# Channel attention with an ELU feed-forward network: thirteen row buffers for batch 0, three early groups of batch 1, and key-query matmuls placed between others

## The chip, the core and the metric

The kernel runs on one core of one Trainium2 chip. The time is device microseconds of one execution; before the change it is 2296.42 us, the median of three runs (2296.3 to 2297.59). The profile is one more execution on the chip, with every instruction's start and end. Engines in it: PE is TensorE's matmul, PEld its weight load, DVE is VectorE, ACT ScalarE, POOL GpSimd, SP SyncE, which issues the DMAs. L12 is line 12 of the kernel.

## The reference

Four batches (B = 4) of N = 6080 rows with C = 256 channels. Attention is over channels: the key-query product is 256 x 256 for a batch and sums over all rows, so nothing of a batch's softmax can start before its last row is there. An ELU network of width 2048 follows.

```python
def _attn_ref(q, k, v, tau) -> np.ndarray:
    qn = q / (np.linalg.norm(q, axis=1, keepdims=True) + 1e-06)
    kn = k / (np.linalg.norm(k, axis=1, keepdims=True) + 1e-06)
    s = kn.transpose(0, 2, 1) @ qn / tau
    s = s - s.max(-1, keepdims=True)
    a = np.exp(s)
    a /= a.sum(-1, keepdims=True) + 1e-09
    return (v @ a).astype(np.float32)

def _moe_ref(x, w_in, w_out) -> np.ndarray:
    h = x @ w_in
    alpha = 1.0
    g = np.where(h > 0.0, h, alpha * (np.exp(np.minimum(h, 0.0)) - 1.0))
    return (g @ w_out).astype(np.float32)
```

Inputs are fp32, the two weight matrices arrive as 64-bit floats.

## The kernel before, in words

The order of the products is changed: for each batch `W' = a @ w_in` (256 x 2048) is made once, and then `h = v @ W'`, the ELU and `g @ w_out` run over the batch's tokens. Most products are split: each fp32 operand becomes a high part and a rest (`split`, a cast on ACT and a subtraction on DVE, L80), and three fast matmuls (high x high, high x rest, rest x high) stand for one. In the head the products are plain fp32 instead; there each matmul shows as two instructions.

**Head (L436 to L502, in an order written out by hand for TensorE and SP).** Rows of q and k come in groups: one group is two rows of every partition, 256 KB of q and 256 KB of k. 6080 rows are 47 a partition and 64 left over; so there are 24 groups, the last of which, `ragged`, has one full row and the 64 left over. `fill_rows` (L116) issues a group's two DMAs from SP; a group of batch 0 is a tile of tag `raw`, of which there are five buffers, so a load waits until the group five before it has been used. For each group TensorE does `multiply` (L432; four fp32 matmuls, eight instructions, 128x256 each), and `square_rows` adds up squares (ACT squares, L143; DVE adds, L144). Products stand `BEHIND` = 2 groups behind the squares in the order. Among the loads are one piece of `w_in` (1 MB) and the first chunk of v (512 KB). After the last square `norms` (L178 to L207) folds the sums, sums them over the partitions by eight small matmuls (L181), takes the root on ACT and makes a scaled identity `dg`; `spread` (L211) multiplies it out; `softmax` and `transpose_a` (L244, copies to `aT` on ACT, L248) follow; `wp_item` (L277) makes the first quarter of W'. The last two groups' products of batch 0 stand behind the norms' matmuls. As a filler, `EARLY` = 2 groups of batch 1 are loaded into a scratch buffer `scr` and multiplied in plain fp32 into a PSUM tile `pe`, partly behind the spread and partly behind the transposes.

The pool tag `wp` has four buffers of 16 KB a partition. Two hold the W' of one batch (`new_wp`), two (`scr`, `scr_r`) serve as scratch in the head and as the next batch's W' later. W' of batch 0 is written at the end of the head and not earlier.

**Main loop (L613 on).** Its steps are pairs (chunk c of 512 or 496 tokens, slice f of 128 of the 2048 hidden channels). A batch has 12 chunks (eight of 512 tokens, then four of 496) of 16 slices. A step is `h_item` (six matmuls, L319 to L321), the ELU on ACT and DVE (`elu`), a split of its result g (L81, L82) and, three steps later (`LAG`), `out_item` (six matmuls, L356 to L358). The first M = 4 chunks go in pieces of slices, because the rest of W' is still being made. Other work is hung on steps: `at(step, fn)` puts it behind the step's own work, `free` ones (the conversions of the weights from 64 bits, `to_f32`) only behind the first softmax (`issue_after(attended)`). For the next batch's attention each group is loaded, squared and split at a step x + 2, and its key-query matmuls (`gram_item`, L157; two 512-wide and two 256-wide for each half of the channels) stand as one run behind the steps x + 4 and x + 5. Outside the head the order on each engine is the scheduler's, from a model of its own and the order of the program as priority.

Of the kernel before, what the change touches and what calls it, by code (L numbers as in the profile page):

```python
# [7 lines left out]
F32 = mybir.dt.float32  # L8
# [20 lines left out]
def channel_attention_then_elu_ffn(ctx: ExitStack, tc, q, k, vT, tau, w_in, w_out, outT):  # L29
# [127 lines left out]
    def gram_item(hl, gram, ct, first, last):  # L157

        pg = gram[ct]
        cs = slice(ct * P, ct * P + P)  # L160
        for r in range(2):
            nc.tensor.matmul(  # L162
                pg, hl[:, 0, 1, r, cs], hl[:, :, 0, r, :], start=(first and r == 0), stop=False
            )
            nc.tensor.matmul(  # L165
# [74 lines left out]
    def transpose_a(b, a):  # L240
# [4 lines left out]
        if b == 0:  # L245
            aT = work.tile([P, KT, C], F32, tag="aT", bufs=1, name=f"aT_{b}")
            for jt in range(KT):
                nc.scalar.copy(aT[:, jt], pt[:, jt])  # L248
        else:
            aT = work.tile([P, 2, KT, C], F32R, tag="aT", bufs=1, name=f"aT_{b}")  # L250
            split(aT[:, 0], aT[:, 1], pt)
# [99 lines left out]
    def out_item(c, f, g, po):  # L351
        n = span(c)[2]
        hi, lo = (g[:, x, 0:n] for x in range(2))
        for dt in range(DT):
            o, ds = po[dt][:, 0:n], slice(dt * P, dt * P + P)
            nc.tensor.matmul(o, wo[:, f, 0, ds], hi, start=first(c, f), stop=False)  # L356
# [55 lines left out]

    scr = work.tile([P, 2 * F], F32, tag="wp", bufs=2 * KT, name="scr")
# [10 lines left out]
    wps[0] = new_wp(0)  # L424
# [11 lines left out]
    with tc.manual_schedule(engines={nc.tensor.engine, nc.sync.engine}):  # L436
        keep_warm(4)

        warm = tiny.tile([P, 1], F32, name="warm")
        nc.scalar.activation(warm, ones[:, 0:1], AF.Square)  # L440
        ragged = work.tile([P, 2, 2, C], F32, tag="g", bufs=4, name="ragged")
        nc.gpsimd.memset(ragged[:, :, 1, :], 0.0)
        fill_rows(ragged, 0, NG - 1)
        gram0 = [pg0[ct][:, 0, :] for ct in range(KT)]
        none = [False] * KT
        multiply(ragged, 0, gram0, [True] * KT, none)
        raws = {x: load_rows(0, x) for x in range(3)}
# [4 lines left out]
        BEHIND = 2  # L452
        FULL = NG - 1
        raw1 = [scratch(x, k=2 * 2).rearrange("p (t r) c -> p t r c", t=2) for x in range(EARLY)]
        for x in range(FULL):
            if x >= BEHIND:
                raw = raws.pop(x - BEHIND)
                for r in range(2):
                    multiply(raw, r, gram0, none, none)
            if x + 3 < FULL:  # L460
                raws[x + 3] = load_rows(0, x + 3)
            if x == 4:
                fill_left(ragged, 0)
            if x == 6:
                wi64[0] = load_w_in(0)
            if x == 14:
                vraw[0] = load_v(0)
# [4 lines left out]
            if x in (11, 14):  # L472
                convert_w_in(0, wi64[0], [(x - 11) // 3])
        for x in range(EARLY):
            fill_rows(raw1[x], 1, x)
        wo64[0] = load_w_out(0)
        pn, dg, rk, nm, ready = norms(0, acc)
        for x in range(FULL - BEHIND, FULL):
            raw = raws.pop(x)
            for r in range(2):  # L480
                multiply(raw, r, gram0, none, [x == FULL - 1 and r == 1] * KT)
# [9 lines left out]

        pe = ps.tile([P, KT, C], F32, tag="o", bufs=8 - KT - WB, name="pe")
        gram1 = [pe[:, ct, :] for ct in range(KT)]
        parts = [(x, r) for x in range(EARLY) for r in range(2)]
        for x, r in parts[:-1]:
            multiply(raw1[x], r, gram1, [x == 0 and r == 0, False], none)
        aT0 = transpose_a(0, a0)
        x, r = parts[-1]
        multiply(raw1[x], r, gram1, none, [False, True])
# [170 lines left out]
```

## Time and profile before

| | us |
|---|---|
| median of three runs | 2296.42 (2296.3 to 2297.59) |
| the profiled execution, own time | 2297.65 |
| its span, first to last instruction | 2295.9 |
| PE busy | 2284.7 |
| DVE busy | 1532.9 |
| ACT busy | 1484.0 |
| DMA | 118.15 MB, mean 51 GB/s |

A busy PE is not PE at its best: matmuls are pipelined, so a matmul's own duration in the profile (0.39 us for a 512-wide one) is longer than its distance to the next start (0.23 us). Where pace matters, read the starts. Rows of the order of time are: start, duration, engine, line, operation, tile written <- tiles read, shape, count of merged instructions, and in brackets the idle time before them and what ended it.

### The profile page before, as it was taken

What the parts mean: (1) busy time and instruction counts of PE and PEld (TensorE: products, weight loads), DVE (VectorE), ACT (ScalarE), POOL (GpSimd) and SP (SyncE); (2) the same over time, 40 slices, a digit from 0 to 9 for tenths busy, and PEclk for the clock granted to TensorE, in tenths of its full rate; (3) what the DMA queues carried; (4) which work ended last, traced back from release to release, by engine and by line L of the source; (5) the groups of instructions that cost most, each with busy time, mean ns of one, the idle gap of its engine ahead of it and who ended that gap; (6) DMA issues with size and microseconds to landing.
All of it is one profiled execution on the core that took longest, in us unless ns stands there. A gap on an engine that the chain in (4) does not pass through costs nothing.

```text
span 2295.9 us, 27137 instructions
## 1 busy us (share of the span) xinstructions
PE 2284.7 (100%) x10232; PEld 1901.1 (83%) x10232; DVE 1532.9 (67%) x2396; ACT 1484.0 (65%) x2425; POOL 3.4 (0%) x11
## 2 busy tenths in 40 slices
PE   8999999999999999999999999999999999999999
PEld 7878888888888888888888888888888888888887
DVE  6995766676766666666666666666666666666665
ACT  6776666666666666666666666666666666666665
POOL 0000000000000000000000000000000000000000
PEclk9999999999999999999999999999999999999999
DMA  9320111110201111111011111121111000000000
GB/s 320 109 74 19 56 65 55 65 62 37 64 19 56 55 46 56 54 48 52 32 60 37 46 47 56 46 64 46 44 37 55 28 19 28 28 19 10 19 9 19
DMA packets 60948, 118.15 MB, mean 51 GB/s; under 512 B 6032, under 2 KB 15760, under 8 KB 60816
## 3 DMA queue, kind: packets, MB, share of 16 engines
q1 hardware_dynamic: 60816, 116.42, 15.0%
q8 instruction: 80, 1.31, 0.2%
q14 instruction: 52, 0.43, 0.1%
HBM read 89.39 MB, written 27.00 MB: 51 GB/s over the span
## 4 chain that ended last, share of the span: by engine, by line
PE 98%; DMA 1%; DVE 0%; SPq 0%; ACT 0%; issue 0%; ACTq 0%
PE ph L319 15%; PE ph L321 15%; PE po L356 15%; PE po L357 15%; PE po L358 15%; PE ph L320 15%; PE gram L162 3%; PE gram L165 1%; DMA raw<-in_k_dram 1%; PE gram L432 1%; PE pw L277 1%; PE pw L281 0%; PE pw L279 0%; PE pw L280 0%; PE pn L181 0%; DMA raw<-in_q_dram 0%
## 5 line engine op out<-in xcount | busy, mean ns | idle before, releaser
L81 ACT CAST g<-e 128x512 fp32r<-128x512 f32 (+1 forms) x768 | 472.2, 615 | 498.1 <-DVE e L336 270.4
L82 DVE TENSOR_TENSOR g<-e,g 128x512 fp32r<-128x512 f32 (+1 forms) x768 | 525.9, 685 | 342.7 <-ACT g L81 296.4
L356 PE MATMUL po<-g,wo 128*128 128x512 f32 (+1 forms) x1536 | 597.2, 389 | 0.0
L357 PE MATMUL po<-g,wo 128*128 128x512 f32 (+1 forms) x1536 | 595.4, 388 | 0.0
L358 PE MATMUL po<-g,wo 128*128 128x512 f32 (+1 forms) x1536 | 594.9, 388 | 0.0
L319 PE MATMUL ph<-vt,wp 128*128 128x512 f32 (+1 forms) x1472 | 574.3, 390 | 0.0
L321 PE MATMUL ph<-vt,wp 128*128 128x512 f32 (+1 forms) x1472 | 571.7, 388 | 0.0
L320 PE MATMUL ph<-vt,wp 128*128 128x512 f32 (+1 forms) x1472 | 570.2, 387 | 0.0
L332 DVE SCALAR_TENSOR_TENSOR e<-e,ph 128x512 f32<-128x512 f32 (+1 forms) x416 | 283.3, 681 | 304.4 <-ACT e L331 303.7
L330 ACT ACTIVATE e<-ph 128x512 f32<-128x512 f32 (+1 forms) x416 | 247.0, 594 | 167.8 <-PE ph L321 165.1
L358 PEld LDWEIGHTS po<-g,wo 128*128 128x128 f32 x1536 | 288.4, 188 | 59.2
L357 PEld LDWEIGHTS po<-g,wo 128*128 128x128 f32 x1536 | 288.4, 188 | 57.9
L356 PEld LDWEIGHTS po<-g,wo 128*128 128x128 f32 x1536 | 288.3, 188 | 56.8
L319 PEld LDWEIGHTS ph<-vt,wp 128*128 128x128 f32 x1472 | 276.4, 188 | 58.1 <-issue 0.7
L321 PEld LDWEIGHTS ph<-vt,wp 128*128 128x128 f32 x1472 | 276.3, 188 | 56.7
L320 PEld LDWEIGHTS ph<-vt,wp 128*128 128x128 f32 x1472 | 276.7, 188 | 50.9 <-issue 0.7
L331 ACT ACTIVATE e<-e 128x512 f32<-128x512 f32 (+1 forms) x416 | 261.3, 628 | 12.2
L334 ACT ACTIVATE e<-ph 128x512 f32<-128x512 f32 (+1 forms) x352 | 208.5, 592 | 83.4 <-PE ph L321 70.0
L336 DVE TENSOR_TENSOR e<-ph,e 128x512 f32<-128x512 f32 (+1 forms) x352 | 241.0, 685 | 10.5
L335 DVE TENSOR_SCALAR e<-e 128x512 f32<-128x512 f32 (+1 forms) x352 | 148.7, 423 | 53.4 <-ACT e L334 53.1
L144 DVE TENSOR_TENSOR acc<-acc,sq 128x1024 f32<-128x1024 f32 x81 | 98.9, 1221 | 13.7 <-ACT sq L143 13.4
L162 PE MATMUL gram<-qk 128*128 128x512 f32 x280 | 103.1, 392 | 0.0
(106 smaller groups left out, 1176.1 us busy)
## 6 DMA issues: line engine op xcount, KB each, us to landing
raw<-in_q_dram SPq DMA_DIRECT2D x90, 256.0 KB, 2.7
raw<-in_k_dram SPq DMA_DIRECT2D x90, 256.0 KB, 2.9
v<-in_v_dram SPq DMA_DIRECT2D x32, 512.0 KB, 3.4
out_dram<-o SPq DMA_DIRECT2D x56, 256.0 KB, 2.0
v<-in_v_dram SPq DMA_DIRECT2D x16, 496.0 KB, 3.4
out_dram<-o SPq DMA_DIRECT2D x32, 248.0 KB, 2.1
wraw<-w_scr SPq DMA_DIRECT2D x12, 512.0 KB, 3.1
wi<-in_moe_w_in_dram SPq DMA_DIRECT2D x4, 1024.0 KB, 6.7
```

The costliest lines, as they stand in the source:

```text
L81: nc.scalar.copy(hi, src)
L82: nc.vector.tensor_sub(lo, src, hi.bitcast(F32))
L319: nc.tensor.matmul(ph[:, 0:n], wp[kt][:, 0, fs], hi, start=(kt == 0), stop=False)
L320: nc.tensor.matmul(ph[:, 0:n], wp[kt][:, 0, fs], lo, start=False, stop=False)
L321: nc.tensor.matmul(ph[:, 0:n], wp[kt][:, 1, fs], hi, start=False, stop=(kt == KT - 1))
L330: nc.scalar.activation(ev, pv, AF.Relu, scale=-1.0)
L331: x = nc.scalar.activation(ev, ev, AF.Exp, scale=-1.0)
L332: y = nc.vector.scalar_tensor_tensor(ev, ev, -1.0, pv, op0=ALU.add, op1=ALU.max)
L336: y = nc.vector.tensor_tensor(ev, pv, ev, op=ALU.max)
L356: nc.tensor.matmul(o, wo[:, f, 0, ds], hi, start=first(c, f), stop=False)
L357: nc.tensor.matmul(o, wo[:, f, 1, ds], hi, start=False, stop=False)
L358: nc.tensor.matmul(o, wo[:, f, 0, ds], lo, start=False, stop=last(c, f))
```

## The change

- Batch 0's groups get thirteen buffers: eight in the two `wp` buffers that W' of batch 0 takes later (`room`; four groups in each), five of tag `raw`. A load of group x + 13 is issued behind the product of group x. `wps[0]` is made only behind the early items.
- The first loads: k of `ragged` and of groups 0 and 1 is issued by ACT, the rest by SP. Order on SP: ragged, groups 0 to 8, the 64 left-over rows, tau, the piece of w_in, groups 9 to 12, then 13 to 22 as buffers come free, then the first chunk of v (before: behind group 17), the early groups, w_out.
- `BEHIND` = 5; the norms' matmuls now stand ahead of the last group's product only. The second product of `ragged` stands where it did, at x = 9, which is now behind group 4's product instead of group 7's.
- `EARLY` = 3 groups of batch 1; their six parts (one row of a group each) go one ahead of the spread, three behind it, two behind the transposes.
- The squares of the early groups move from behind the softmax to the main loop's steps 1, 2 and 3; what waited for the softmax's last DVE instruction now waits, on ACT, for the last copy to `aT` too.
- `gram_item` becomes a generator; `out_item` issues one of its four matmuls behind each of its own first four. The two halves stand at steps x + 5 and x + 6 instead of behind x + 4 and x + 5.

```diff
-    EARLY = 2
-
-    def fill_rows(raw, b, g):
+    EARLY = 3
+
+    def fill_rows(raw, b, g, queues=(nc.sync, nc.sync)):
...
-            nc.sync.dma_start(
+            queues[t].dma_start(
...
     def gram_item(hl, gram, ct, first, last):
...
-            nc.tensor.matmul(
+            yield nc.tensor.matmul(
                 pg, hl[:, 0, 1, r, cs], hl[:, :, 0, r, :], start=(first and r == 0), stop=False
             )
-            nc.tensor.matmul(
+            yield nc.tensor.matmul(
                 pg[:, 0, :], hl[:, 1, 1, r, cs], hl[:, 0, 0, r, :], start=False, stop=(last and r == 1)
             )
...
-    def out_item(c, f, g, po):
+    def out_item(c, f, g, po, between):
...
             nc.tensor.matmul(o, wo[:, f, 0, ds], hi, start=first(c, f), stop=False)
+            next(between, None)
             nc.tensor.matmul(o, wo[:, f, 1, ds], hi, start=False, stop=False)
+            next(between, None)
             nc.tensor.matmul(o, wo[:, f, 0, ds], lo, start=False, stop=last(c, f))
+            next(between, None)
...
+    room = [work.tile([P, 2 * F], F32, tag="wp", bufs=2 * KT, name=f"room_{x}") for x in range(KT)]
...
+        BEHIND = 5
+        FULL = NG - 1
+        EACH = 2 * F // (2 * KT * C)
+        DEEP = KT * EACH + 5
...
+        def load0(x):
+
+            y = x % DEEP
+            if y < KT * EACH:
+                n = 2 * KT * C
+                raws[x] = room[y // EACH][:, y % EACH * n : (y % EACH + 1) * n].rearrange(
+                    "p (t r c) -> p t r c", t=2, r=2
+                )
+            else:
+                raws[x] = work.tile([P, 2, 2, C], F32, tag="raw", bufs=5, name=f"raw_0_{x}")
+            fill_rows(raws[x], 0, x, (nc.sync, nc.scalar if x < 2 else nc.sync))
+
+        fill_rows(ragged, 0, NG - 1, (nc.sync, nc.scalar))
+        multiply(ragged, 0, gram0, [True] * KT, none)
+        for x in range(3):
+            load0(x)
...
+        for x in range(3, 9):
+            load0(x)
+        fill_left(ragged, 0)
...
+        wi64[0] = load_w_in(0)
+        for x in range(9, DEEP):
+            load0(x)
...
+        def gram0_item(x):
+            raw = raws.pop(x)
+            for r in range(2):
+                multiply(raw, r, gram0, none, [x == FULL - 1 and r == 1] * KT)
+            if x + DEEP < FULL:
+                load0(x + DEEP)
+
         for x in range(FULL):
             if x >= BEHIND:
-                raw = raws.pop(x - BEHIND)
-                for r in range(2):
-                    multiply(raw, r, gram0, none, none)
-            if x + 3 < FULL:
-                raws[x + 3] = load_rows(0, x + 3)
...
+                gram0_item(x - BEHIND)
             square_rows(raws[x], acc, x == 0, sq1 if x % 2 else None)
             if x == 9:
                 square_rows(ragged, acc, False)
                 multiply(ragged, 1, gram0, none, none)
-            if x in (11, 14):
-                convert_w_in(0, wi64[0], [(x - 11) // 3])
+            if x in (12, 15):
+                convert_w_in(0, wi64[0], [(x - 12) // 3])
+        vraw[0] = load_v(0)
         for x in range(EARLY):
             fill_rows(raw1[x], 1, x)
         wo64[0] = load_w_out(0)
+        for x in range(FULL - BEHIND, FULL - 1):
+            gram0_item(x)
         pn, dg, rk, nm, ready = norms(0, acc)
-        for x in range(FULL - BEHIND, FULL):
...
+        gram0_item(FULL - 1)
...
+        early_items(1)
         spread(pn, dg)
...
+        early_items(3)
+        wps[0] = new_wp(0)
+        aT0, copied = transpose_a(0, a0)
+        attended = (attended, copied)
+        early_items(2 * EARLY - 4)
...
-    with tc.issue_after(attended):
+    with tc.issue_after(attended[0]), tc.issue_after(attended[1]):
         convert_w_out(0, wo64[0])
         nc.scalar.copy(early, pe)
-        for x in range(EARLY):
-            square_rows(raw1[x], acc1, x == 0)
...
+    for x in range(EARLY):
+        at(1 + x, lambda x=x: square_rows(raw1[x], acc1, x == 0))
...
-            at(x + 4, lambda b=b, g=g: gram(b, g, 0))
-            at(x + 5, lambda b=b, g=g: gram(b, g, 1))
+            for ct in range(KT):
+                fine[x + 5 + ct] = gram(b, g, ct)
...
-            out_item(c, f, gs.pop(j), pos[c])
+            out_item(c, f, gs.pop(j), pos[c], fine.pop(i, iter(())))
```

`early_items(n)` issues the next n parts of the early groups; a part is the product of one row of a group, two fp32 matmuls.

More of the change, by code (lines that the diff above doesn't have):

```diff
@@ L584, in gram @@
             g0 = first_group(b)
-            gram_item(state[b, "hl", g], state[b, "gram"], ct, g == g0, g == NG - 1)
+            yield from gram_item(state[b, "hl", g], state[b, "gram"], ct, g == g0, g == NG - 1)
         def soft(b):
@@ L629, in channel_attention_then_elu_ffn @@
                 ]
-            out_item(c, f, gs.pop(j), pos[c])
+            out_item(c, f, gs.pop(j), pos[c], fine.pop(i, iter(())))
             if last(c, f):
                 store(c, f, pos.pop(c))
-        with tc.issue_after(attended):
+        with tc.issue_after(attended[0]), tc.issue_after(attended[1]):
             for fn in loose.get(i, ()):
```

48 lines of the change are left out of this document (17 added, 31 removed).

## The prediction

> **What bounds the kernel now.** I read the page's totals first, then the span cut into windows, then TensorE's instructions in order of time.
>
> ```profile
> span 2295.9 us, 27137 instructions
> PE 2284.7 (100%) x10232; PEld 1901.1 (83%) x10232; DVE 1532.9 (67%) x2396; ACT 1484.0 (65%) x2425; POOL 3.4 (0%) x11
> ```
>
> TensorE is the whole path: 11 us of the span are without a matmul. An edit can pay only where TensorE idles, where its clock is down, or where its matmuls follow each other more slowly than their width asks for. The first two lie in the head:
>
> ```profile
> 27.00:45.60 18.60, 18.60 (x87) 16.15 (x85) 17.47 (x21) 13.60 (x15) 0.00 (x0) 1.00 0.93 321
> 45.60:50.70 5.10, 0.14 (x1) 0.00 (x0) 3.33 (x4) 2.58 (x3) 0.00 (x0) 0.95 0.97 320
> 50.70:57.00 6.30, 6.22 (x19) 5.33 (x20) 2.85 (x12) 4.11 (x6) 0.00 (x0) 0.50 1.04 409
> ```
>
> Columns: the window, its length, busy time of PE, weight loads, DVE, ACT, POOL, then granted clock, DMA share, GB/s. TensorE is packed until 45.6, idles 5 us, and then runs 6.3 us at half clock. What it does and waits for, in order of time:
>
> ```profile
> 50.77 1.86 PE L181 MATMUL pn<-ones,acc 128*128 128x1 f32 x8 [5.04 <-DVE acc L178]
> 52.50 5.90 PE L432 MATMUL gram<-raw 128*128 128x256 f32 x16
> 58.24 0.59 PE L211 MATMUL pn<-dg,ones 128*128 128x256 f32 x2
> 58.67 2.75 PE L432 MATMUL pe<-scr 128*128 128x256 f32 x12
> 61.26 0.60 PE L244 MATMUL pt<-ident,a 128*128 128x128 f32 x4
> 62.56 0.81 PE L277 MATMUL pw<-wf,aT 128*128 128x256 f32 x3
> ```
>
> ```profile
> 42.74 4.83 DMA raw<-in_k_dram
> 47.68 1.06 ACT sq L143
> 48.77 1.24 DVE acc L144
> 50.03 0.70 DVE acc L178
> ```
>
> The second fence is the chain of waits. The last k rows land at 47.57; square, addition and fold take 3 us more, and the norm matmuls stand in TensorE's queue ahead of the last two groups' products. So the load bounds the head's end. The product is nearly as long: the twelve instructions from 58.67 to 61.26 are 0.216 us apart, a group of two rows is eight of them (an fp32 matmul is two), 1.73 us. What idling costs beside the wait: the sixteen at 52.50 take until 58.24, 5.74 us, where 16 x 0.216 is 3.46.
>
> The third place is the main loop. In these rows the first column is the start:
>
> ```profile
> 708.93 0.39 PE L319 MATMUL ph<-vt,wp 128*128 128x512 f32 x1
> ...
> 711.65 0.39 PE L162 MATMUL gram<-qk 128*128 128x512 f32 x1
> 711.88 0.28 PE L165 MATMUL gram<-qk 128*128 128x256 f32 x1
> 712.00 0.40 PE L162 MATMUL gram<-qk 128*128 128x512 f32 x1
> 712.23 0.28 PE L165 MATMUL gram<-qk 128*128 128x256 f32 x1
> 712.35 0.40 PE L319 MATMUL ph<-vt,wp 128*128 128x512 f32 x1
> 712.59 0.40 PE L320 MATMUL ph<-vt,wp 128*128 128x512 f32 x1
> ...
> 715.13 0.39 PE L162 MATMUL gram<-qk 128*128 128x512 f32 x1
> ```
>
> A step's twelve 512-wide matmuls take 2.72 us (708.93 to 711.65), 0.227 each; a 256-wide one takes 0.12. After a run of four key-query matmuls the next twelve take 2.78 (712.35 to 715.13), the first of them 0.24, and the run itself 0.70 where 2 x 0.227 + 2 x 0.1135 is 0.68. One run costs about 0.08 us beyond its width. In the 496-wide chunks the slow pace does not end; a step inside the key-query stage takes 2.68 us, one after it 2.64:
>
> ```profile
> 520.04 0.39 PE L319 MATMUL ph<-vt,wp 128*128 128x496 f32 x1
> ...
> 522.72 0.38 PE L319 MATMUL ph<-vt,wp 128*128 128x496 f32 x1
> ```
>
> ```profile
> 612.91 0.38 PE L319 MATMUL ph<-vt,wp 128*128 128x496 f32 x1
> ...
> 615.55 0.38 PE L319 MATMUL ph<-vt,wp 128*128 128x496 f32 x1
> ```
>
> ```profile
> L162 PE MATMUL gram<-qk 128*128 128x512 f32 x280 | 103.1, 392 | 0.0
> ```
>
> 280 records, two to a run, are 140 runs. Some two thirds fall among 512-wide chunks (eight of a batch's twelve), 93 x 0.08 = 7 us; the others leave about 48 steps of each of three batches slow, 144 x 0.04 = 6 us. So about 13 us of the span hang on how these matmuls stand among the others.
>
> **The change, part by part.** *Thirteen buffers.* The loads no longer wait for a buffer, and the first v chunk goes behind all of batch 0's rows. How the rate goes with the queue:
>
> ```profile
> 2.00:9.00 7.00, 6.19 (x17) 4.52 (x16) 0.22 (x1) 2.33 (x4) 0.00 (x0) 1.00 0.90 274
> 30.00:48.00 18.00, 15.74 (x73) 13.50 (x72) 15.98 (x18) 12.32 (x14) 0.00 (x0) 1.00 0.92 305
> ```
>
> 305 GB/s with at most five groups under way, 409 (50.7 to 57.0, above) with the weight loads queued behind them. I take 400 from 9 us on, as the deep queue is the new case. The ragged tail now lies behind nine groups: 2 x 128 KB, 18 x 256 KB and 2 x 64 KB are 5.1 MB, and some 0.5 MB of later loads will be partly moved by then: 9 + (5.6 - 1.9)/0.4 = 18.2 us; with k's first three loads issued by ACT I take 17.7 (17.0 to 18.5). TensorE has done groups 0 to 4 by then and waits about a microsecond, because the ragged product now stands ahead of group 5. From there it has 4 + 17 x 8 = 140 instructions to the norms, 30.2 us: 47.9. The last rows (14 groups and w_in, 8.4 MB more) land at 38.7.
>
> VectorE is then later than the load. Its conversion of half a w_in piece is three instructions of the first and three of the second kind here, 3.3 us:
>
> ```profile
> 25.78 0.42 DVE L97 TENSOR_SCALAR cv<-cv 128x512 f32<-128x512 f32 x1
> ...
> 26.70 0.69 DVE L100 SCALAR_TENSOR_TENSOR cv<-wi,cv 128x512 uint32<-128x512 uint32 x1
> ```
>
> From group 9 on (landed 21.9, squared by 23.0) it has 15 additions of 1.24 and two conversions, 25 us, of which up to 3 fit in while w_in arrives. acc is done between 45 and 48, plus 0.70: 47.2 by the middle, so TensorE's 47.9 decides; 48.7 at worst.
>
> Behind it TensorE is packed and keeps its clock: norms 8 x 0.108 (half of what 50.77 to 52.50 shows at half clock) 0.87, last group 1.73, four early instructions 0.86, spread 0.43, twelve early 2.59, transposes 0.44, eight early 1.73, together 8.65: first W' matmul at 56.55 instead of 62.56. The softmax between spread and transposes had 2.59 us (58.67 to 61.26) and has as much. **-6.0 us** (-3.5 to -7.5).
>
> The Trainium skill speaks against the 400: "DMA: Bandwidth & Descriptors", section "Where 436 GB/s comes from", has loads from HBM bound at about 358 GB/s for a core. By that figure W' would begin some 1.6 us later, at 58.2. The window with 409 GB/s disagrees, so the sum keeps 400.
>
> *Third early group.* Its eight fp32 instructions are in the sum above, as a filler under the softmax. Later eight matmuls fall out, 4 x 0.227 + 4 x 0.115: **-1.4 us**, and with them their splits.
>
> *Squares moved.* Three squares of ACT (1.06 each) and two additions of DVE now stand in steps 1 to 3 of the main loop instead of under the softmax, and ACT's part of the w_out conversion waits for the aT copies.
>
> ```profile
> 70.00:80.00 10.00, 10.00 (x46) 8.14 (x45) 9.97 (x20) 9.46 (x19) 0.00 (x0) 1.00 0.46 157
> ```
>
> ```profile
> 70.90 0.68 DVE L82 TENSOR_TENSOR g<-e,g 128x512 fp32r<-128x512 f32 x1
> ```
>
> ```profile
> 71.59 0.39 PE L356 MATMUL po<-g,wo 128*128 128x512 f32 x1
> ```
>
> DVE and ACT are full there, and the first g ends at 71.58, the moment its first out matmul starts; its low half is read two matmuls later. No cover is left: up to 3.2 us if all of it is paid, nothing if the scheduler defers the conversions. The sums free VectorE about a microsecond earlier relative to W', so I take **+1.0** (0 to 3.2).
>
> *Spread.* The same matmuls in another order: 512, 256, 512, 256 become separated by out matmuls, with three 512-wide ones between two 256-wide. Ends: 0 and -13; or, if each lone 256 keeps the slow pace alive, +2. The nearest row is the first 256 of a run: it and its forerunner go at full pace, and the slow begins behind it. Three spacers are more than one, but recovery above took a whole step. I take half, **-6**.
>
> Sum: -6.0 - 1.4 + 1.0 - 6 = -12.4. The profiled execution took 2297.65 (1.75 around its span); the median of the runs is 1.23 less: 2296.42 - 12.4 = **2284.0 us**.
>
> **Rivals.** (1) *The order doesn't matter.* Then the head alone counts: 2290.0. For: a lone 256 among 512s is nowhere in the trace. Against: the pace differs exactly behind runs. The Trainium skill leans this way ("TensorE: Matmul & The Clock Gate", Part 2): weight loads are pulled ahead of running matmuls, and 128 columns load in 128/1.2 = 107 ns, less than a 256-wide matmul takes; by that the order costs nothing either way.
> (2) *The head isn't shortened enough.* If the queue gives 305 GB/s all along, the tail lands at 21.1, the last rows at 48.7, acc and fold end at 51.7, W' begins at 60.3: 3.7 us of the gain are gone, 2287.7. For: 274 GB/s at the start, where loads were queued too.
> (3) *Slower.* The first v chunk now lands at 40 us, 512 KB behind the last rows. ScalarE's queue is in order. If its cast (some 1.1 us) stands ahead of square 9, squares and conversions start adding at 42.2, and 15 x 1.24 + 6.7 put acc at 67.5, W' at 67.5 + 0.7 + 8.65 + 3.4 (half clock) = 80.2: 17.7 us late instead of 6.0 early, 2308. From square 14 on it would be no loss. Against: before, the load stood between two rows' loads in SP's order and the cast between the same two squares.
>
> **How the numbers follow.** Forecast 55% (own range 2278 to 2288), order without effect 25%, head not shortened 12%, slower 8%. What can be told from no change is about 0.2%, 4.6 us: below 2291.8 lie the forecast, most of rival 1 and most of rival 2. Faster 0.80, same 0.12, slower 0.08. The low end takes the whole 13 us of the order and the rest as it is, 2277; the high end rival 1 with the stall at its full 3.2 and a little of the head lost, 2293.
>
> **What would show it.** No TensorE idle above 1.5 us between 18 us and W', and clock 1.00 from 45 to 60; DMA at 400 GB/s from 9 to 45 us; W' at 56 to 57; the step behind key-query matmuls at 2.72 us; no idle PE in the first eight steps. Wrong: an idle ACT before a v cast, PE waits at steps 1 to 8, or the 2.68 us step still there.

## The result, and the profile after

| | before | after |
|---|---|---|
| median | 2297.44 us (2294.93 to 2298.62, 12 runs) | 2291.14 us (2289.16 to 2292.87, 12 runs) |
| profiled execution, own time | 2297.65 | 2291.67 |
| W' of batch 0 begins | 62.56 | 59.86 |
| step 31 begins | 153.56 | 151.91 |
| batch 1 begins (step 192) | 636.83 | 633.45 |
| batch 2 begins (step 384) | 1203.89 | 1199.22 |
| span | 2295.9 | 2289.9 |

The changed kernel is faster, ratio 0.9973 (95% interval 0.9964 to 0.9981), 6.3 us: half of the 12.4 forecast. Line numbers have moved: `multiply` is L439, the norms' matmuls L184, the spread L214, the transposes L247, W' L280, the key-query matmuls L165 and L168, h from L322, the out matmuls L360 to L364. The page's totals after:

```profile
span 2289.9 us, 27116 instructions
PE 2280.6 (100%) x10232; PEld 1899.0 (83%) x10232; DVE 1533.7 (67%) x2395; ACT 1480.5 (65%) x2424; POOL 3.1 (0%) x11
```

TensorE still is the whole path: 9 us of the span are without a matmul, 11 before, and the number of its instructions is the same. So the gain is read from when its marks come. Before and then after, the first h matmul of step 31 and of batch 1 (first column: start):

```profile
153.56 0.39 PE L319 MATMUL ph<-scr_r,wp 128*128 128x512 f32 x1
...
636.83 0.39 PE L319 MATMUL ph<-vt,wp 128*128 128x512 f32 x1
```

```profile
151.91 0.39 PE L322 MATMUL ph<-scr_r,wp 128*128 128x512 f32 x1
...
633.45 0.39 PE L322 MATMUL ph<-vt,wp 128*128 128x512 f32 x1
```

The head gives 2.70 us (62.56 to 59.86), the first 31 steps take back 1.05 (1.65 left), batch 0's stage then gives 1.73 (3.38 in all), the next one 1.29 (4.67), and the third 1.31 (1770.96 before against 1764.98 after, at step 576); the last batch, without key-query work, gives nothing. TensorE's head in order of time, after:

```profile
8.38 7.17 PE L439 MATMUL gram<-room 128*128 128x256 f32 x32 [0.57 <-DMA room<-in_k_dram]
18.79 1.10 PE L439 MATMUL gram<-ragged 128*128 128x256 f32 x4 [3.23 <-DMA ragged<-in_k_dram]
...
50.77 0.95 PE L184 MATMUL pn<-ones,acc 128*128 128x1 f32 x8
51.58 1.97 PE L439 MATMUL gram<-raw 128*128 128x256 f32 x8
53.39 1.03 PE L439 MATMUL pe<-scr 128*128 128x256 f32 x4
54.25 0.59 PE L214 MATMUL pn<-dg,ones 128*128 128x256 f32 x2
54.68 2.75 PE L439 MATMUL pe<-scr 128*128 128x256 f32 x12
57.34 0.95 PE L247 MATMUL pt<-ident,a 128*128 128x128 f32 x4
58.13 1.89 PE L439 MATMUL pe<-scr 128*128 128x256 f32 x8
59.86 3.40 PE L280 MATMUL pw<-wf,aT 128*128 128x256 f32 x15
```

The 5.04 us of waiting ahead of the norms are gone; in their place TensorE waits 3.23 us at 15.6 us for the ragged group's left-over rows. The windows after (columns as before: length, busy PE, weight loads, DVE, ACT, POOL, clock, DMA share, GB/s):

```profile
15.40:18.70 3.30, 0.16 (x1) 0.00 (x0) 3.04 (x3) 2.42 (x3) 0.00 (x0) 1.00 1.01 333
20.10:23.50 3.40, 3.40 (x10) 2.68 (x9) 0.69 (x3) 1.72 (x2) 0.00 (x0) 0.50 1.04 392
23.50:45.60 22.10, 22.10 (x104) 19.41 (x104) 21.16 (x25) 14.33 (x14) 0.00 (x0) 1.00 1.03 384
45.60:50.77 5.17, 5.17 (x26) 4.55 (x24) 3.31 (x4) 3.37 (x4) 0.00 (x0) 1.00 1.04 407
```

Behind that wait the granted clock is 0.50 from 20.11 to 23.52, which costs half of 3.41 us, 1.7. From there to W' TensorE is packed at full clock. The loads move 384 to 407 GB/s there, where they moved 321 before; from 9.00 to 18.70 us they move 348.

### The profile page after: what moved, and what is told of

Same layout as the page of the kernel before. It is cut to its first block, busy times and chain, and to the rows that moved or that the text cites. A ratio compares the mean times of both kernels' runs of the same rounds, so it can differ in the third digit from the quotient of the medians.

```text
span 2289.9 us, 27116 instructions
## 1 busy us (share of the span) xinstructions
PE 2280.6 (100%) x10232; PEld 1899.0 (83%) x10232; DVE 1533.7 (67%) x2395; ACT 1480.5 (65%) x2424; POOL 3.1 (0%) x11
## 3 DMA queue, kind: packets, MB, share of 16 engines
q8 instruction: 80, 1.31, 0.2%
## 4 chain that ended last, share of the span: by engine, by line
PE 98%; DMA 1%; ACT 0%; DVE 0%; issue 0%; ACTq 0%; SPq 0%; DVEq 0%
PE ph L322 15%; PE po L364 15%; PE po L360 15%; PE po L362 15%; PE ph L324 15%; PE ph L323 15%; PE gram L165 3%; PE gram L439 1%; PE gram L168 1%; PE pw L280 1%; DMA room<-in_k_dram 0%; PE pw L284 0%; PE pw L283 0%; PE pw L282 0%; DMA ragged<-in_k_dram 0%; PE pn L184 0%
## 5 line engine op out<-in xcount | busy, mean ns | idle before, releaser
L360 PE MATMUL po<-g,wo 128*128 128x512 f32 (+1 forms) x1536 | 596.0, 388 | 0.2 <-ACT g L81 0.2
L364 PE MATMUL po<-g,wo 128*128 128x512 f32 (+1 forms) x1536 | 596.0, 388 | 0.0
L322 PE MATMUL ph<-vt,wp 128*128 128x512 f32 (+1 forms) x1472 | 573.6, 390 | 0.0
L360 PEld LDWEIGHTS po<-g,wo 128*128 128x128 f32 x1536 | 288.4, 188 | 58.2 <-ACT g L81 0.7
L364 PEld LDWEIGHTS po<-g,wo 128*128 128x128 f32 x1536 | 288.4, 188 | 52.3 <-DVE g L82 0.4
L322 PEld LDWEIGHTS ph<-vt,wp 128*128 128x128 f32 x1472 | 276.3, 188 | 56.6 <-PE po L364 0.6
L165 PE MATMUL gram<-qk 128*128 128x512 f32 x276 | 108.5, 393 | 0.0
```

The costliest lines, as they stand in the source:

```text
L322: nc.tensor.matmul(ph[:, 0:n], wp[kt][:, 0, fs], hi, start=(kt == 0), stop=False)
```

## The experiments

All are edits of the changed kernel, and each is given with the kernel before timed on the same chip (2297.45, 2297.64, 2297.59 and 2297.41 us in the four sittings). "Left at step 31" is how much earlier than before that step begins in the trace.

### Do the buffers make the head shorter?

**Nine buffers** (four groups in the room of W' and five of `raw`, instead of eight and five):

```diff
-        DEEP = KT * EACH + 5
+        DEEP = 4 + 5
...
-            if y < KT * EACH:
+            if y < DEEP - 5:
```

> The changed kernel with nine buffers for batch 0's groups instead of thirteen (one of the two W' buffers, and the five). Theory from the changed kernel's trace: SP issues a load only when the eighth load before it has landed (33.47 behind 33.40, 34.06 behind 34.04), so no more than four groups are ever under way and buffers beyond some nine do nothing: last rows at 41, W' between 57.5 and 60, 2291. Rival (the deep queue is what shortened the head): last rows at 43 or later, W' 1.5 us later, 2293.

2290.74 us (2289.04 to 2291.05), ratio 0.9968 (0.9956 to 0.9981). The last k rows land at 40.99 (40.95 with thirteen), W' begins at 59.10. The buffers beyond nine do nothing for the time.

**Five buffers**, as before the change, with the order of the products after it (the left-over rows, tau and w_in are issued behind group 4):

```diff
-        DEEP = KT * EACH + 5
+        DEEP = 0 + 5
...
-        for x in range(3, 9):
+        for x in range(3, 5):
             load0(x)
```

> The changed kernel with the five buffers of before; the 64 left-over rows, tau and the piece of w_in are then loaded behind group 4. Theory (the head's end is set by VectorE's additions, 1.33 us apart, and not by the load): last rows at 43 to 45, sums folded at 49 to 50, no wait for the ragged tail at 15 us, W' between 58 and 60.5, 2291. Rival (the buffers made the head's gain): last rows at 47 as before, W' at 60.5 or later, 2292.5 or more.

2290.37 us (2288.89 to 2292.72), ratio 0.9969 (0.9958 to 0.998). Without the added room the head is no longer: W' begins at 58.18. The last rows land 3.65 us later than with thirteen, at 44.60, and the norms come 3 us earlier, because the wait at 15 us and its half clock are missing and the sums end at 47.74 instead of 49.15. TensorE's order of time in this kernel, all that waits between 12 us and W':

```profile
47.80 1.05 PE L184 MATMUL pn<-ones,acc 128*128 128x1 f32 x8 [0.96 <-DVE acc L181]
52.44 0.70 PE L214 MATMUL pn<-dg,ones 128*128 128x256 f32 x2 [0.89 <-DVE dg L208]
```

What shortened the head is the order, not the buffers. That is the order of the products (all but one group ahead of the norms) and of the loads (the first v chunk behind all rows) together: with the same five buffers the last rows land 2.97 us earlier than in the kernel before. No run separates the two. Why so many buffers don't help is in the issues of the changed kernel: its page's row gives KB of each and the median time to landing, SyncE's order of time the pace:

```profile
room<-in_q_dram SPq DMA_DIRECT2D x16, 256.0 KB, 5.1
```

```profile
30.17 0.33 SPq L119 DMA_DIRECT2D room<-in_k_dram  x1
30.89 0.33 SPq L119 DMA_DIRECT2D room<-in_q_dram  x1
31.47 0.33 SPq L119 DMA_DIRECT2D room<-in_k_dram  x1
```

One load each 0.65 us and 5.1 us to land are eight loads, four groups, under way; more than eight never are in these traces, however many buffers are free. The chain of waits shows it at the start too: the load issued at 8.36 follows the landing, at 8.34, of one issued at 1.65. The rate does hang on the room up to there: from 20 to 40 us it is 317 GB/s with five buffers, 357 with nine and 382 with thirteen.

### The wait at 15 us and the clock

**Tail later**: the second ragged product at x = 14 instead of 9.

```diff
                 square_rows(ragged, acc, False)
+            if x == 14:
                 multiply(ragged, 1, gram0, none, none)
```

> The changed kernel with the second ragged product behind group 9's product instead of group 4's; nothing else. Theory (the wait for the ragged tail and the half clock it sets off are what the head lost): no PE idle between 9 and 45 us, clock 1.00 throughout, batch 0's products up to the norms done at 45.7 instead of 50.8; then the norms wait for acc, which in the changed kernel was folded at 49.1, so W' begins at 57.8 to 58.2 instead of 59.86, and the time falls by 1.6 to 2 us to about 2289.3. Rival (the load is the bound and the wait only moves): the idle time reappears at a later group, W' at 59.9, 2291.1.

2291.44 us (2288.35 to 2293.54), ratio 0.9973 (0.9964 to 0.9982): nothing gained. The wait at 15 us went, and one for the sums came. The order of time and a window of this kernel:

```profile
49.22 1.51 PE L184 MATMUL pn<-ones,acc 128*128 128x1 f32 x8 [1.82 <-DVE acc L181]
```

```profile
49.65:56.45 6.80, 6.80 (x20) 5.63 (x20) 3.11 (x12) 1.66 (x3) 0.00 (x0) 0.50 1.03 408
```

TensorE came to the norms earlier than VectorE's sums, waited 1.82 us and lost the clock for 6.8 us, and W' began at 61.35. So the sums bound the head as soon as the first wait is gone. Their pace in the changed kernel, in VectorE's order of time:

```profile
23.13 0.43 DVE L97 TENSOR_SCALAR cv<-cv 128x512 f32<-128x512 f32 x1 [2.71 <-ACT cv L94]
...
45.88 1.23 DVE L144 TENSOR_TENSOR acc<-acc,scr 128x1024 f32<-128x1024 f32 x1
47.20 1.23 DVE L144 TENSOR_TENSOR acc<-acc,sq 128x1024 f32<-128x1024 f32 x1
48.46 0.69 DVE L181 TENSOR_TENSOR acc<-acc 128x512 f32<-128x512 f32 x1
```

The additions stand 1.32 us apart, not 1.24, because ScalarE's next square waits for the buffer that the addition frees, and VectorE had been idle for 2.71 us at 20.4.

**Head filled**: the tail as above, and the six early parts put where TensorE would wait: two ahead of the norms, one ahead of the spread, three behind it, none behind the transposes.

```diff
+            if x == 14:
                 multiply(ragged, 1, gram0, none, none)
...
+        early_items(2)
+        pn, dg, rk, nm, ready = norms(0, acc)
+        gram0_item(FULL - 1)
...
-        early_items(2 * EARLY - 4)
```

> The changed kernel with the second ragged product behind group 9's (as in e1) and two of the six early parts moved from behind the transposes to ahead of the norms, where e1's TensorE waited for the sums. Theory (TensorE's clock falls when it waits about 2 us or more inside one 3.4 us period; without such waits the head ends when the sums allow): no half clock between 9 us and the end, W' at 56.5 to 57.2. But the first steps are bound by VectorE and ACT (with two early groups W' began 6.1 us earlier than before, and 3.8 were left behind step 31), so only 3.6 to 4.0 us are left behind step 31, and the time is 2289 to 2289.5. Rival (TensorE bounds the first steps): all of the 5.5 to 6 us stay, 2287.

2289.04 us (2288.76 to 2290.15), ratio 0.9965 (0.9952 to 0.9977). Its order of time:

```profile
47.82 1.05 PE L184 MATMUL pn<-ones,acc 128*128 128x1 f32 x8 [0.37 <-DVE acc L181]
...
55.92 3.72 PE L280 MATMUL pw<-wf,aT 128*128 128x256 f32 x16 [0.46 <-ACT aT L251]
```

The clock stays full, and W' begins at 55.92, ahead of the 56.55 forecast. But of these 6.64 us only 4.48 are left at step 31.

**GpSimd's help for the sums**: on top of that kernel, the squares of every third group (x = 2, 5, ...) are added up by GpSimd in a sum of its own, which VectorE adds at the end.

```diff
+            if x % 3 == 2:
...
+                    nc.scalar.activation(sqp, raws[x], AF.Square)
+                    nc.gpsimd.tensor_add(accp, accp, sqp)
+            else:
+                square_rows(raws[x], acc, x == 0, sq1 if x % 2 else None)
...
+        nc.vector.tensor_add(acc, acc, accp)
```

> e7 with every third group's squares added up by POOL in a sum of its own, which VectorE adds at the end: seven additions of VectorE fewer, one more. Theory (VectorE's additions set the end of the sums): sums folded at 45 or earlier instead of 47 to 48.5, W' 1 us earlier than in e7; but with the first steps bound by VectorE and ACT no more than 4 us are left behind step 31: 2289. Rival (the last rows' landing sets it): sums folded as in e7.

2299.35 us (2296.38 to 2300.47), ratio 1.0008 (0.9999 to 1.0017): 10 us worse than without. GpSimd's and then VectorE's order of time:

```profile
35.16 3.03 POOL L504 TENSOR_TENSOR aT_p<-aT_p,o_p 128x1024 f32<-128x1024 f32 x1 [5.86 <-ACT o_p L503]
41.38 2.44 POOL L504 TENSOR_TENSOR aT_p<-aT_p,o_p 128x1024 f32<-128x1024 f32 x1 [3.19 <-ACT o_p L503]
```

```profile
36.00 3.27 DVE L144 TENSOR_TENSOR acc<-acc,scr 128x1024 f32<-128x1024 f32 x1
...
41.65 3.25 DVE L144 TENSOR_TENSOR acc<-acc,sq 128x1024 f32<-128x1024 f32 x1
```

VectorE's addition issued at 36.00 ends at 39.27, 1.08 us after GpSimd's ends (38.19); the one at 41.65 ends at 44.90, 1.08 after 43.82. The three others that were issued under one of GpSimd's end 1.08 or 1.09 us after it too. It doesn't run slower, it stands until the other is done. The sums end at 55.31, TensorE waits 6.85 us and W' begins at 65.55.

### What the first steps take back

**Squares early**: the early groups' squares behind the softmax again.

```diff
+    with tc.issue_after(attended[0]):
+        for x in range(EARLY):
+            square_rows(raw1[x], acc1, x == 0)
...
-    for x in range(EARLY):
-        at(1 + x, lambda x=x: square_rows(raw1[x], acc1, x == 0))
```

> The changed kernel with the squares of the early groups written right behind the softmax again instead of in steps 1 to 3. Theory (these squares fill ACT and VectorE where nothing covers them, and cost the 1.05 us that the marks lose between steps 3 and 32): the steps lose 0 to 0.3, 2290.1. Rival (the loss is that ACT's part of the conversions now starts behind the copies to aT): the marks lose 1 us all the same, 2291.1.

2291.79 us (2290.12 to 2293.39), ratio 0.9974 (0.9965 to 0.9984). W' begins 3.76 us earlier than before, and 2.06 are left at step 31: 1.70 lost, not less than the 1.05 with the squares moved. Moving them is not what the first steps pay for; the time is that of the rival in the expectation, by which ScalarE's part of the w_out conversion costs it, since that now waits for the copies to `aT`. The traces show where this comes from. ScalarE's first instruction of the conversion and VectorE's, before and then after:

```profile
56.17 0.65 ACT L94 ACTIVATE cv<-wo 128x512 f32<-128x512 f32 x1
61.40 0.41 DVE L97 TENSOR_SCALAR cv<-cv 128x512 f32<-128x512 f32 x1
```

```profile
58.86 0.68 ACT L94 ACTIVATE cv<-wo 128x512 f32<-128x512 f32 x1
59.57 0.43 DVE L97 TENSOR_SCALAR cv<-cv 128x512 f32<-128x512 f32 x1 [1.48 <-ACT cv L94]
```

Before, ScalarE had its part done ahead of the softmax's end, and VectorE began 0.14 us behind the first transpose (61.26). After, ScalarE begins behind the copies, and VectorE stands idle for 1.48 us and begins 2.23 behind the first transpose (57.34). Step 31 begins 92.30 us behind the first transpose before and 94.56 after. Over the kernels the two go together: where VectorE begins 2.23 us behind it, step 31 comes 94.47 to 94.72 behind it; in the two where it begins 1.89 and 1.93 behind (the one with the tail later and the one with GpSimd's help), 94.25 and 94.26. With the squares early it is 95.21. No run moves the conversion alone, so this cause rests on the traces.

**Two early groups**: `EARLY` = 2, all else as changed.

```diff
-    EARLY = 3
+    EARLY = 2
```

> The changed kernel with two early groups instead of three. Prediction on record: the third is worth 1.4 us, as its fp32 products only fill TensorE's waits. Theory: they are not free, since TensorE is packed from the norms to W': without them W' begins about 0.9 us earlier, steps 1 to 32 lose about 0.5 us less, and batch 1's key-query stage is 1.5 us longer: 2291.1 + 0.1, no change that can be told. If the prediction's step holds, 2292.5.

2290.36 us (2289.01 to 2293.9), ratio 0.9971 (0.996 to 0.9982), the time of the changed kernel. The third group costs TensorE eight instructions in the head, 1.73 us, and W' begins at 56.47 without them, 6.09 earlier than before; at step 31 3.77 are left, 2.32 lost. But counted from the first transpose, step 31 comes no earlier without the group (94.72 us, 94.56 with it): its products behind the transposes fill time that the first steps don't need. Nor does the loss grow with how early the head ends. It is 0.95 to 1.08 in the nine kernels that have the squares moved and two early parts behind the transposes, where W' comes 1.2 to 5.0 us earlier than before, and 2.14 to 2.32 in the four that have none, though in one of these (GpSimd's help) W' comes 3.0 us later. W' is only a poor mark: without parts behind the transposes it begins sooner, and what the first steps wait for doesn't. From 70 to 80 us VectorE and ScalarE are busy for 10.00 of 10 us after the change, and TensorE has 42 matmuls, where the kernel before has 46 (in the prediction). So what starts late behind the softmax isn't made up there.

### The order of the key-query matmuls

**In runs**: as before the change, four behind steps x + 4 and x + 5.

```diff
-                fine[x + 5 + ct] = gram(b, g, ct)
+                at(x + 4 + ct, lambda b=b, g=g, ct=ct: list(gram(b, g, ct)))
```

> The changed kernel with the key-query matmuls again as runs of four behind steps x + 4 and x + 5. Theory from the marks of the two traces (batch 2 and batch 3 each 1.3 us shorter, batch 1 0.35 beside the third group): spreading is worth 3 us, so 2294. Prediction on record: 6 us, 2297. Rival (order is worth nothing, the shorter batches come from other things): 2291.1. The step behind a run is then 2.78 us again, the 496-wide step 2.68.

2293.39 us (2292.53 to 2293.91), ratio 0.998 (0.9971 to 0.9988). The spread is worth 2.3 us in the times. In the traces, from step 31 to the end, the changed kernel gains 4.33 on the kernel before (1.65 to 5.98) and this one 0.93 (3.28 to 4.21): 3.40 for the order alone. The times differ by less, which fits the head of this trace: it kept its clock there, and step 31 begins 1.63 us earlier than in the changed kernel.

**All wide**: the 256-wide product takes both halves of q, 512 wide. It computes one more, small term.

```diff
-                pg[:, 0, :], hl[:, 1, 1, r, cs], hl[:, 0, 0, r, :], start=False, stop=(last and r == 1)
+                pg, hl[:, 1, 1, r, cs], hl[:, :, 0, r, :], start=False, stop=(last and r == 1)
```

> The changed kernel with the 256-wide key-query matmuls made 512 wide (the rest of k times both parts of q, one more small term of the product). Width alone adds 66 groups x 4 x 0.1135 us = 30 us. Theory (the slow stretches are set off by the short matmuls): every step inside the key-query stages takes 2.72 us (512) or 2.64 us (496) beside its key-query matmuls, some 10 us of slow pace are gone, 2311. Rival (any key-query matmul sets it off, through its tiles or the work beside it): slow stretches stay, 2321.

2313.14 us (2312.04 to 2314.51), ratio 1.0067 (1.0053 to 1.008). The added width costs more than the slow pace ever did, but the slow pace is gone: what the matmuls from 250 us on take beyond their widths is some 1 us in its trace, against 10.0 in the changed kernel (summed as in the table below). It is the narrow matmuls that set it off.

**Narrow ones in a row**: a group's eight as one run at x + 5, four 512 wide and then four 256 wide.

```diff
-            for ct in range(KT):
-                fine[x + 5 + ct] = gram(b, g, ct)
+            at(x + 5, lambda b=b, g=g: grams(b, g))
```

> The changed kernel with a group's eight key-query matmuls as one run behind step x + 5, the four 512-wide first and then the four 256-wide back to back. Theory (each 256-wide matmul leaves a debt of its own, about 35 ns, which the 512-wide ones behind it pay): the slow stretch behind the run is twice as long, 24 matmuls or so, and the time is that of the runs of four, about 2294. Rival (a slow stretch of a dozen matmuls follows however many short ones there were): half of the cost in the 512-wide chunks goes, 3 us or so under the runs of four, about 2291.

2289.14 us (2288.11 to 2289.54), ratio 0.9962 (0.9949 to 0.9976). The order of time behind such a run, among 512-wide chunks:

```profile
707.62 1.07 PE L626 MATMUL gram<-qk 128*128 128x512 f32 x4
708.52 0.64 PE L631 MATMUL gram<-qk 128*128 128x256 f32 x4
709.00 0.40 PE L322 MATMUL ph<-vt,wp 128*128 128x512 f32 x1
...
711.74 0.39 PE L322 MATMUL ph<-vt,wp 128*128 128x512 f32 x1
...
714.46 0.39 PE L322 MATMUL ph<-vt,wp 128*128 128x512 f32 x1
```

The run takes 1.38 us where its widths ask for 1.36, the step behind it 2.74, the next 2.72: 0.04 us for a whole group. So four narrow matmuls one behind another leave no more slow ones behind them than one does. What costs is each change from narrow back to wide. In the changed kernel the same place reads (h's first matmul of four steps; the key-query matmuls stand in the first two):

```profile
708.26 0.39 PE L322 MATMUL ph<-vt,wp 128*128 128x512 f32 x1
...
711.70 0.40 PE L322 MATMUL ph<-vt,wp 128*128 128x512 f32 x1
...
715.17 0.40 PE L322 MATMUL ph<-vt,wp 128*128 128x512 f32 x1
...
717.92 0.39 PE L322 MATMUL ph<-vt,wp 128*128 128x512 f32 x1
```

3.44, 3.47 and 2.75 us, where 3.40, 3.40 and 2.72 are clean: 0.14 for a group, against two times 0.08 of before. Spreading saved next to nothing here. Among 496-wide chunks it is the other way round. After, the starts of a clean step, of two with key-query matmuls, of a clean one and of the next:

```profile
1045.71 0.38 PE L322 MATMUL ph<-vt,wp 128*128 128x496 f32 x1
...
1048.35 0.38 PE L322 MATMUL ph<-vt,wp 128*128 128x496 f32 x1
...
1051.69 0.39 PE L322 MATMUL ph<-vt,wp 128*128 128x496 f32 x1
...
1055.07 0.38 PE L322 MATMUL ph<-vt,wp 128*128 128x496 f32 x1
...
1057.71 0.38 PE L322 MATMUL ph<-vt,wp 128*128 128x496 f32 x1
```

2.64, then 3.34 and 3.38 (3.32 would be clean), then 2.64 again: the slow 2.68 us step of before is gone here. The table sums over the matmuls from 250 us on the distance to the next start less the clean one (2.72/12 us for 512, 2.64/12 for 496, half of the first for 256); the few that stand next to the softmaxes' small matmuls are left out:

| us beyond width | 512-wide | 496-wide | key-query | all |
|---|---|---|---|---|
| before | 6.3 | 5.3 | 1.6 | 13.2 |
| after (spread) | 5.4 | 2.9 | 1.7 | 10.0 |
| in runs | 6.3 | 5.9 | 1.6 | 13.7 |
| narrow in a row | 1.3 | 6.1 | 1.7 | 9.1 |
| by width (next) | 1.4 | 3.4 | 1.5 | 6.2 |

**Order by width**: the run of eight where the chunk is 512 wide, the spread where it is 496 wide.

```diff
+            if span(steps[x + 5][0])[2] == CH:
+                at(x + 5, lambda b=b, g=g: grams(b, g))
+                continue
             for ct in range(KT):
                 fine[x + 5 + ct] = gram(b, g, ct)
```

> The changed kernel with the run of eight of e4 at steps of 512-wide chunks, and the matmuls spread as in the changed kernel at steps of 496-wide chunks. Sums of the starts' distances beyond the width from 250 us on: before 13.2 us (512-wide 6.3, 496-wide 5.3, the key-query matmuls 1.6), changed 10.0 (5.4, 2.9, 1.7), run of eight 9.1 (1.3, 6.1, 1.7). Theory (what each order saves it saves in its own chunks): 1.3 + 2.9 + 1.5, some 5.7, so 4.3 under the changed kernel, 2286.8. Rival (the pace inside the 496-wide chunks depends on how they are entered): the 496-wide part is 6 again, 2289.

2287.74 us (2285.61 to 2288.09), ratio 0.9955 (0.9943 to 0.9968), 3.4 us below the changed kernel, although W' begins at 60.28 in its trace (half clock from 17.20 to 24.03). The two savings add, as the table shows.

**Even widths**: narrow in a row, and chunks of 508 and 506 tokens instead of 512 and 496, to be rid of the 496.

```diff
-    unit = 16 if n % 16 == 0 else 2
+    unit = 2
```

> e4 with a batch cut into chunks of 508 and 506 tokens instead of 512 and 496; the same columns in all. Theory (the slow pace is about 223 ns to a matmul at least, so it ends by itself where the width asks for more, 506 x 0.4434 = 224.4, and never does at 496, 219.9): the slow part of the four last chunks shrinks from 6.1 to some 2 us, 2285 to 2286. Rival (slow stretches end for another reason than width, or widths that aren't multiples of 16 cost of their own): 2289 or more.

2306.67 us (2305.47 to 2307.89), ratio 1.004 (1.0026 to 1.0054). A step of 506-wide matmuls, in the last batch, far from any key-query work:

```profile
2000.47 0.39 PE L322 MATMUL ph<-vt,wp 128*128 128x506 f32 x1
...
2003.19 0.39 PE L322 MATMUL ph<-vt,wp 128*128 128x506 f32 x1
```

2.72 us, to the hundredth what 512-wide ones take. 256 of the 768 steps had been 496 wide at 2.64; at 2.72 they cost 20 us more, which covers the 17.5 lost on the kernel with the narrow ones in a row. The theory of this run fell.

### Both together

The filled head with the order by width, since each was faster than the changed kernel by itself:

> The head of e7_head_filled (second ragged product later, two early parts ahead of the norms, none behind the transposes) together with the order of e11_order_by_width (key-query matmuls of a group as one run, four wide and then four narrow, in the 512-wide chunks, and one behind each of four out matmuls in the 496-wide ones). Each was faster than the kernel before by itself: 2289.04 with W' begun at 55.92, and 2287.74 with W' begun at 60.28. Theory (the two gains lie in different stages and add up): the head puts step 31 about 4.5 us earlier than before, the order saves about 7.3 us from there to the end, together 11.8: 2285.8 us (2284 to 2287). Rival (the main loop gives the head's time back, because VectorE and ScalarE set its first steps and the conversions come due at the same time): 2287.5 to 2288.5, no better than the order alone. What tells them apart besides the time: step 31 at -4.5 or at -3 against before.

2285.67 us (2285.48 to 2285.88), ratio 0.9949 (0.9935 to 0.9962): 11.7 us under the kernel before and 5.5 under the changed one. Step 31 begins at 149.56, 4.00 us earlier than before, and the span ends at 2283.7, 12.2 earlier: the gains add up (4.48 at step 31 in the kernel with the head filled; 8.35 from there on in the one with the order by width, 8.19 here). Its runs lie within 0.4 us of each other, those of the changed kernel within 3.7; without a long wait in the head there is no clock to lose.

## Why half of it came

**Head, predicted -6.0, came -2.70.** The step that failed is "waits about a microsecond, because the ragged product now stands ahead of group 5", and with it "keeps its clock". The left-over rows landed at 18.66 (17.7 predicted, the worst of the range 18.5); TensorE was done with group 4 at 15.56, about a microsecond sooner than the prediction has it. So the wait was 3.23 us, and it took the clock with it: the norms began 2.87 us late, 1.1 from the landing and 1.75 of half clock (the 140 instructions took 31.98 us instead of 30.2). The rest, 50.77 to 59.86, is 9.09 us against 8.65. A second term was mis-sized behind it: the sums, with 47.2 predicted and 48.7 as the worst, were done at 49.15. TensorE was later, so they cost nothing in this kernel, and 1.8 us plus the clock in the one with the tail later; with these sums the norms would have begun 1.25 us late without any wait at 15 us, too. The "400 from 9 us on, as the deep queue" were 348 GB/s until 18.70, by itself enough to bring the left-over rows a microsecond late, and 384 to 407 from 20 us on. More than eight loads are never under way, however many buffers there are, and the kernel with five, at 317 GB/s, has the same time. The windows from 20 us on also speak against the 358 GB/s for a core which the Trainium skill has in "DMA: Bandwidth & Descriptors". (By the sum's own 3.7 MB, 358 instead of 400 GB/s would have moved the wait's end and W' by 1.1 us, not by the 1.6 that the prediction gives.)

**First steps, predicted +1.0, came +1.05.** The prediction names two causes, the moved squares and the w_out conversion that waits for the copies to `aT`. The squares are not it: with them back behind the softmax 1.70 were lost. The conversion fits the traces, though no run moves it alone: VectorE begins it 2.09 us later behind the first transpose than before, and step 31 comes 2.26 later behind it. That the number was met is in part luck: counted from the first transpose the head gave 3.92 us (61.26 to 57.34) and the stretch to step 31 took 2.26 back, and which part of that is booked on the head hangs on the early parts that stand ahead of W'.

**Third early group, predicted -1.4.** In batch 0's stage, where its matmuls fall out, the kernel with runs gains 1.34 on the kernel before (3.28 at step 31 to 4.62 at step 192), so the term had its size there. In the two stages behind it loses 0.41 again (4.21 at the end) at an unchanged order, for a reason that no run shows; 0.93 are left. The pair with and without the group, both spread, differs by 0.6 in batch 0's stage (1.73 against 1.12). At step 31 it costs nothing. The times of the pair (2291.14 with, 2290.36 without) mix this with the head's clock: the trace without the group waits 1.51 us for the left-over rows and keeps its clock.

**Spread, predicted -6, came -3.4.** "I take half" was right in sign and wrong in where: among 512-wide chunks it kept nearly all of the slow pace (each lone narrow matmul sets off its own stretch, the case priced at +2), among 496-wide ones it ended what had not ended before. The step behind key-query matmuls is not 2.72 there but 2.75.

The terms as measured: -2.70 + 1.05 - 0.93 - 3.40 = -5.98, the traces' difference.

**What was to show it.** The clock was 1.00 from 45 to 60 us, as predicted, and in the first eight steps TensorE's order of time has one wait, 0.23 us at 74.07 for a g; the loss there shows as fewer matmuls in the window, not as waits. 400 GB/s from 9 us, W' at 56 to 57 and the clean step behind key-query matmuls were each missed as above. The sign for idle time looked only behind 18 us, and 2.4 of the 3.23 us of the wait lay ahead of it.

**The rivals.** That the order doesn't matter fell with the pair of orders, and with it what the prediction drew from the Trainium skill ("TensorE: Matmul & The Clock Gate", Part 2), that weight loads pulled ahead make the order free: the same matmuls span 7.5 us more or less by it (13.7 against 6.2 in the table). That the head isn't shortened enough came nearly true in its time of W' (60.3, measured 59.86), but not by its mechanism: at 305 GB/s the left-over rows were to land at 21.1, and they landed at 18.66. The slower case did not come: the cast of v stood behind the last square.

## What to carry to other kernels

A head in which one engine waits for a late load is mended by putting any other ready work in front of the waiting instruction, and each wait that remains has to be priced with the clock it may cost, not with its own length. Count the gain from the point where the next stretch's bound begins, and not from a handy mark: here step 31 followed the first transpose at a fixed distance, whatever stood between that and W'. Where VectorE and ScalarE are full behind the head, look at what the change makes them start later before the gain is booked in whole. Where matmuls of two widths mix, count the changes of width, and try the order in each stage by itself.

## What the runs showed of the hardware

- The clock is taken in steps of 3.41 us (20.11 to 23.52 after, 49.65 to 56.48 with the tail later), at a phase that differs between executions. A wait well under that length is enough, but how it falls on these periods matters more than its length: 1.82 us took the clock with the tail later, 1.84 us left it at 1.00 in the kernel with runs, and so did 2.48 us in the one with the narrow ones in a row, where the wait was split over two periods that TensorE filled to 0.57 and 0.70. In the kernel with runs the period was filled to 0.46 and with the tail later to 0.47, so the bound lies about there, and these runs don't place it closer. The half clock then lasted for one period (in the changed kernel) or two (with the tail later); what decides that is not shown. The Trainium skill ("TensorE: Matmul & The Clock Gate", Part 1) has a free-running window of 3413 ns, which agrees, and names an idle window as what throttles; here a half idle one did.
- A change from a 256-wide to a 512-wide matmul is followed by a slow stretch; behind a run of four narrow ones the next six h matmuls took 0.23 instead of 0.227 us each. Among 496-wide ones it lasts until something ends it; what does so in the spread order stays open.
- A matmul of 506 columns takes as long as one of 512. 496 is 31 x 16, so the width seems to be rounded up to a multiple of 16 (or 8), or other widths have a cost of their own; which of them was not measured.
- VectorE's addition of two tiles in SBUF stands still while GpSimd adds two others, to the end of GpSimd's instruction. The Trainium skill ("SBUF — State Buffer", "Who interferes with whom") says so: a VectorE instruction with two SBUF inputs contends with a GpSimd instruction that reads SBUF, and the one that is issued later is blocked for the whole length of the other. The 1.08 us in both pairs above, where GpSimd's was issued first, agree.
